# A state-space scan ahead of a feed-forward layer: the first group of tokens, taken as one block or as two halves

## The chip, the cores and the metric

The kernel runs on one core of a Trainium2 chip. The metric is device time in microseconds (us), the median of several executions. A profile is one execution on the same kind of core, recorded instruction by instruction; its "span" runs from the first to the last instruction of the program.

A core has several engines, each with its own instruction stream that it works off in order: TensorE (PE in the profile; its weight loads are listed apart as PEld), VectorE (DVE), ScalarE (ACT), GpSimd (POOL) and SyncE (SP), which here mainly issues DMAs. They meet through semaphores. This kernel fixes the order on every engine by hand: at its end a helper, `in_order`, ties each instruction to the one that the program text emitted before it on the same engine. So a line that stands earlier in the text is earlier in its engine's queue, and an instruction that waits holds up all that stand behind it on that engine.

## The reference, cut to what matters

Two layers in a row. The first (Mamba2, "ssd") works on x (4 batches, 8 heads, 768 tokens, 32 channels), a decay `a` per token and head, and B, C (16 states per token). In chunks, with `state` carried from chunk to chunk:

```python
L = exp(cum_i - cum_j), causal        # decay inside the chunk
y_intra = ((C B^T) * L) @ x           # inside the chunk
y_inter = (C @ state) * exp(cum)      # from the state before the chunk
state = decay_full * state + sum_j B_j x_j decay_from_j
y = y_intra + y_inter
```

The second layer takes y as 3072 tokens by 256 features: `h = y @ w_in` (256 by 2048), `g = h * sigmoid(1.702 h)`, `out = g @ w_out` (2048 by 256). The weights arrive as 64-bit floats and are turned into fp32 on the chip.

## The kernel before, in words

**Tiling.** The 3072 tokens are six groups of 512. A group is two pairs of 256 tokens (`PG` = 2 pairs per group), a pair is two blocks of 128 tokens, and a block has two sides of 64 tokens. So the scan's chunk is 64 tokens here, four chunks per pair, counted m = 0 to 3. Group 0 is handled by code of its own at the start of the kernel; the change touches only that.

**Feed-forward of group 0.** `hidden(0, f)` (L832) is the first product for slice f of 16 slices of 128 hidden features: weight slices `w_in[:, f, k]`, k = 0 and 1, times `yT[0]`, 512 tokens in two halves of 256. fp32 matmuls appear as two records each, so one f is 8 PE records. All 16 run in a row; after a slice a list of other work (`in_hidden[0]`) is emitted. `project_all(0)` is the second product. Later groups use a cheaper scheme for both products, and are not touched.

**Start of group 0**, in the text's order, L1139 to L1169:

- `ends_first` (DVE) scales B. `fetch(1, held=True)` writes one element of the weight buffer on DVE (L171), so that SP's DMA of piece 1 has to wait for it; `fetch(2)` to `fetch(5)` and `rows_a` (the decays of all tokens) follow on SP. The weights come in pieces: 0 to 3 are 512 KB with two slices f each, 4 and 5 are 1 MB with four; pieces 6 to 9 are `w_out`.
- `score` (PE, L640) computes C B^T for both pairs. Between the pairs stand `since_first` (PE L501, ACT L506), the first step of unpacking piece 0 (`unpack`, ACT L197), `weigh(0)` (DVE L651: decay times score), `gain` (PE L671: what each chunk adds to the state, for both pairs) and `parts_first` (ACT L690, four copies 128 x 128 into `steps`).
- Then the second step of `unpack(0)` (ACT L200), `shift(0)` (DVE L204), `weigh(1)`, `drops` (POOL L511: the chunk decays), `since_start` (POOL L625, two: C times decay, "CsT"), and `keep_first` (DVE L695): one scan of 512 elements that turns the increments of all eight chunks into states. `sign(0)` and `join(0)` (DVE L209, L223) finish weight piece 0.
- `dense(2)` (PE L1117) are two matmuls of ones whose result nobody reads.
- `finish(range(PG))` writes y of both pairs into four PSUM banks: first `intra` for pair 0 and pair 1 (L787, 64 records each), then, feature half t by feature half t, `inter` for both pairs (L775, 56 records in all; chunk 0 has no state before it) and two ACT copies (L804) into `yT[0]`.
- `table(AF.Silu)` loads ACT's table, `unpack(2)` and `narrow(1)` (shift, sign, join of piece 1) follow, and `hidden(0, 0)` begins.

PSUM tiles named through `bank` come from four rotating banks, so a new one waits until the reader of the fourth one back is done. `area` is one larger PSUM area with a single buffer.

SP's queue is worked off in the same way: after the pieces come `rows_a`, `fetch(6)` (called by `join(1)`), then the loads for the next group at slice 1 (`load`), and at slice 6 `store_a`, `fetch(7)`, more loads, `fetch(8)`, `fetch(9)`, and at slice 9 the `spread` loads from `scratch`.

Of the kernel before, what the change touches and what calls it, by code (L numbers as in the profile page):

```python
# [8 lines left out]
FP32 = mybir.dt.float32  # L9
U32 = mybir.dt.uint32  # L10
BF16 = mybir.dt.bfloat16
AF = mybir.ActivationFunctionType
# [24 lines left out]
def kernel(  # L37
# [125 lines left out]
    def fetch(i, held=False):  # L163
        name, f, n = PIECES[i]
        if n == 2 and f % 4:
            t = pieces.pop(i - 1)[:, 2 * n * DM:]
        else:
            t = pieces[i] = words(f"bits{i}")
            t = t[:, :2 * n * DM]
        if held:  # L170
            nc.vector.memset(t[:, :1], 0)  # L171
        if name == "in":
            src = moe_w_in[:, 2 * f * P:2 * (f + n) * P].rearrange("(k p) e -> p k e", p=P)
            dst, src = (v.rearrange(s, h=n, e=2 * P) for v, s in (
                (t, "p (h k e) -> k p h e"), (src, "p k (h e) -> k p h e")))
# [278 lines left out]
    def ends_first(p):  # L454

        t = ssd.tile([P, R, 2 * Q, N], FP32, tag="Be", name=f"Be{p}", bufs=3)
        nc.vector.tensor_tensor(
            out=t, in0=rb[p],
            in1=flat[p].rearrange("p r (e i) -> p r e i", i=H)[:, :, :, H - 1:H].to_broadcast(
                [P, R, 2 * Q, N]), op=ALU.mult)  # L460
        BE[p] = t.rearrange("p r (k q) n -> p k r (q n)", k=2), t
# [44 lines left out]
            nc.scalar.activation(since[0][:, 2 * p:2 * p + 2].rearrange("p c s -> p (c s)"),  # L506
                                 rows[p], AF.Exp)

    def drops():

        nc.gpsimd.tensor_copy(  # L511
            drop[:, :, 1:], since[0][:, :CG].rearrange("p c (s i) -> p (c s) i", s=2)[:, 1:, H - 1].unsqueeze(
                1).to_broadcast([P, Q * D, 2 * CG - 1]))

    def fan_since():
        o = bank("rows4")
# [49 lines left out]
    def bank(name):  # L566
        return ps.tile([P, 4 * P], FP32, tag="ff", name=name)

    def area(name):
        return psa.tile([P, R, 4 * P], FP32, tag="cb", name=name)  # L570
# [88 lines left out]
    def gain(pairs, to=None):  # L659
# [16 lines left out]
                            skip_group_check=True)  # L676
            increment[p] = [t[:, 2 * n:2 * n + 2] for t in A] if pairs[0] else A

    steps = const.tile([P, Q * D, 2 * CG], FP32, name="steps")
    drop = ffn.tile([P, 4, TG // 2], FP32, tag="my", name="drop", bufs=1)[:, :2].rearrange(  # L680
        "p a (e m) -> p (a e) m", m=2 * CG)
    nc.gpsimd.memset(drop[:, :, 0:1], 0.0)

    def parts_first():

        to = steps.rearrange("p (q d) (c s) -> p s q c d", s=2, q=Q)
        for i in range(2):
            o = increment[0][i].rearrange("p c (q d) -> p q c d", q=Q)
            for q in range(Q):
                nc.scalar.activation(to[:, i, q], o[:, q], AF.Copy, scale=part[:, q:q + 1])  # L690

    def keep_first():

        flat_steps = steps.rearrange("p e m -> p (e m)")
        nc.vector.tensor_tensor_scan(  # L695
            out=flat_steps, data0=drop.rearrange("p e m -> p (e m)"), data1=flat_steps,
            initial=0.0, op0=ALU.mult, op1=ALU.add)
        for p in range(PG):
            state[p] = steps.rearrange("p e m -> p m e")[:, 4 * p:4 * p + 4]

    def keep_both(pairs, by_scalar=False):

# [25 lines left out]
    def add_up(p, ms):  # L728
        b, c = divmod(2 * p, NC)
        new = state[p]  # L730
        for m in ms:
            if 2 * c + m > 0 and not last_chunk(p, m):
# [4 lines left out]
                    out=new[:, m], in0=old, scalar=since[b][:, c + k, e:e + 1],  # L737
                    in1=new[:, m], op0=ALU.mult, op1=ALU.add)

    begun_y = {}  # L740

    def finish(pairs, steps=range(2)):


        g, first = divmod(pairs[0], PG)
        early = pairs[0] < PG
        if 0 in steps:
            if early:
                y = [bank(f"y0_{i}")[:, :2 * P].rearrange("p (k i) -> p k i", i=H) for i in range(4)]
                begun_y[0] = [[y[2 * t + i] for t in range(NK)] for i in range(2)], set()  # L750
            else:
                both = area(f"y{pairs[0]}")[:, :, :len(pairs) * 2 * H].rearrange(
                    "p (s t) (k i) -> p s t k i", s=2, i=H)
                begun_y[pairs[0]] = [[both[:, i, t] for t in range(NK)] for i in range(2)] + [both], set()
        y, begun = begun_y[pairs[0]]

        def begin(i, t, parts):
            new = not begun & {(i, t, q) for q in parts}
            begun.update((i, t, q) for q in parts)
            return new  # L760

        def inter(n, p, ts=range(2)):

            for k in range(2):
                for i in range(2):
                    m = 2 * k + i
                    if (4 * p + m) % (2 * NC) == 0:
                        continue
                    old = state[p][:, m - 1] if m else state[p - 1][:, 3]
                    for r in range(R):  # L770
                        t = r // 2
                        if t not in ts:
                            continue
                        rows, to = slice(32 * r, 32 * r + 32), Q * D * (r % 2)
                        nc.tensor.matmul(  # L775
                            out=y[i][t][to:to + Q * D, 2 * n + k], lhsT=old[rows],
                            rhs=st[p]["CsT"][rows, k, SIDES[i]],
                            start=begin(i, t, range(Q * (r % 2), Q * (r % 2) + Q)), stop=early,
                            tile_position=(32 * r, to), skip_group_check=True)

        def intra(n, p):
            L = Ls[p]
            for k in range(2):
                for h in range(NH):
                    t, q = divmod(h, HB)
                    for i, side in enumerate(SIDES):
                        nc.tensor.matmul(  # L787
                            out=y[i][t][D * q:D * q + D, 2 * n + k], lhsT=rx[p][side, k, h],
                            rhs=L[side, k, h // Q, h % Q],
                            start=begin(i, t, (q,)), stop=not early, tile_position=(H * i, D * q),  # L790
                            skip_group_check=True)

        cols = slice(2 * first * P, 2 * (first + len(pairs)) * P)

        if first == 0:
            yT[g] = ffn.tile([P, NK, TG], FP32, tag="yT", name=f"yT{g}")
        if early:
            for n, p in enumerate(pairs):
                intra(n, p)
            for t in range(NK):  # L800
                for n, p in enumerate(pairs):
                    inter(n, p, (t,))
                for i in range(2):
                    nc.scalar.activation(  # L804
                        yT[g][:, t, cols].rearrange("p (k s i) -> p s k i", s=2, i=H)[:, i], y[i][t],
                        AF.Copy)
        else:
            for step in steps:
                for n, p in enumerate(pairs):
                    (inter, intra)[step](n, p)  # L810
            if 1 not in steps:
                return
            for i in range(2):
                nc.scalar.activation(  # L814
                    yT[g][:, :, cols].rearrange("p t (k s i) -> p s t k i", s=2, i=H)[:, i], y[2][:, i],
                    AF.Copy)
        for p in pairs:
            state.pop(p - 1, None)
            st.pop(p)
            Ls.pop(p)  # L820
# [5 lines left out]
    def block(g, j):  # L826
        if g or j < 6:
            gT[g, j] = ffn.tile([P, 2, TG], FP32, tag="gT", name=f"gT{g}_{j}", bufs=6)
        else:
            gT[g, j] = ffn.tile([P, 2, TG], FP32, tag="mg", name=f"gT{g}_{j}", bufs=3)  # L830

    def hidden(g, f):  # L832
        j, i = divmod(f, 2)
# [304 lines left out]
    turn_back()  # L1138
    ends_first(0)  # L1139
    ends_first(1)  # L1140
    fetch(1, held=True)
    for i in range(2, 6):
        fetch(i)
    rows_a(az, (nc.sync,))

    def between_scores():
        since_first()
        unpack(0, (0,))
        weigh(0)
        gain(range(PG))  # L1150
        parts_first()

    score(range(PG), between_scores)
    unpack(0, (1,))
    shift(0)
    weigh(1)
    drops()
    for p in range(PG):
        since_start(p, nc.gpsimd)
    keep_first()  # L1160
    sign(0)
    dense(2)
    unpack(1)
    finish(range(PG))
    dense(0)
    join(0)
    table(AF.Silu)
    unpack(2)
    narrow(1)  # L1169


    def at(places, i, *work):
# [46 lines left out]


    for f in range(NF):
        hidden(0, f)
        for do in in_hidden[0].get(f, []):
            do()
    project_all(0, in_project[0])
# [177 lines left out]
```

## Time and profile before

| what | value |
|---|---|
| median of 3 runs | 355.07 us (355.07 to 355.61) |
| the profiled execution: its time / its span | 356.2 / 354.2 us |
| PE / PEld busy | 346.6 (98%) / 300.9 us (85%) |
| DVE / ACT / POOL busy | 241.5 (68%) / 150.0 (42%) / 14.0 us (4%) |
| first matmul of `hidden(0, 0)` starts | 22.07 us |
| 16 slices of `hidden(0, f)`, span of their records | 22.1 to 53.9 us |

The profile has a page (busy shares, the span in forty slices, the chain of work that ended last, the costliest groups) and views of the trace: a timeline for one engine and window, a table by windows with busy time and granted TensorE clock, a view by source line, a view of waits, and the DMA queues. In a timeline row the columns are start, duration, engine, line, operation, output and inputs, shapes, count, and in brackets the idle time before it with what ended it; "issue" there means that the engine waited for nothing that the profile shows.

### The profile page before, as it was taken

The page shows a single profiled execution, that of the slowest core. Times are in us where ns is not written, and L with a number is a line of the kernel's source. Part 1 is how long each engine was busy: PE and PEld are TensorE (multiplying, and loading weights), DVE is VectorE, ACT ScalarE, POOL GpSimd, SP SyncE. Part 2 cuts the span into 40 slices and gives each one's busy share as a digit, 9 for nine tenths or more (in the row PEclk, how much of TensorE's full clock was granted, in tenths as well). Part 3 has the DMA queues.
Part 4 walks back from the last instruction along what each step waited for, and adds up shares of the span by engine and source line. Part 5 has one row for each costly group of instructions (what it writes and reads, how often), then busy time and mean ns, then how long its engine had stood idle before and what let it go on. Part 6 is the DMA issues. An engine that isn't in the chain of part 4 may idle for free.

```text
span 354.2 us, 8373 instructions
## 1 busy us (share of the span) xinstructions
PE 346.6 (98%) x3506; PEld 300.9 (85%) x3506; DVE 241.5 (68%) x453; ACT 150.0 (42%) x346; POOL 14.0 (4%) x42
## 2 busy tenths in 40 slices
PE   8799999999999999999999999999999999999996
PEld 6578888888888888888888888888888888889996
DVE  5635798779867999666898476789374555465463
ACT  4657757013563331654333454333454331553320
POOL 8400000100000100000000000000000000000000
PEclk9969999999999999999999999999999999999999
DMA  6897799552544500415614016400000310000401
GB/s 129 227 304 159 190 241 202 98 89 42 104 71 92 104 0 2 68 41 119 121 30 76 0 34 131 82 11 2 1 4 3 45 16 0 0 2 0 59 2 59
DMA packets 87100, 26.19 MB, mean 74 GB/s; under 512 B 69528, under 2 KB 84248, under 8 KB 87064
## 3 DMA queue, kind: packets, MB, share of 16 engines
q1 hardware_dynamic: 86232, 25.15, 34.4%
q10 hardware_dynamic: 832, 0.52, 0.6%
q8 instruction: 27, 0.44, 0.5%
q14 instruction: 9, 0.07, 0.1%
HBM read 22.41 MB, written 3.24 MB: 72 GB/s over the span
## 4 chain that ended last, share of the span: by engine, by line
PE 88%; DVE 4%; DMA 3%; SPq 2%; issue 2%; ACT 0%; POOL 0%; DVEq 0%; POOLq 0%; ACTq 0%
PE acc L1006 25%; PE X L899 17%; PE Y L909 13%; PE h L843 11%; PE o L943 8%; PE acc L1013 7%; PE y L775 2%; PE y L787 2%; PE cb L640 2%; DMA a<-scratch 1%; DMA bits<-in_moe_w_in_dram 1%; PE A L671 1%; DVE mw L966 1%; DVE gT L1033 1%; SPq L150 1%
## 5 line engine op out<-in xcount | busy, mean ns | idle before, releaser
L904 ACT ACTIVATE ac<-X 128x256 f32<-128x256 f32 x76 | 29.1, 383 | 78.6 <-PE X L899 78.2
L1006 PE MATMUL acc<-mg,mw 128*128 128x256 f32 x192 | 54.5, 379 | 0.0
L876 ACT ACTIVATE gT<-gT 128x512 f32<-128x512 f32 (+1 forms) x76 | 39.3, 519 | 34.3 <-DVE gT L1033 33.7
L1033 DVE TENSOR_TENSOR gT<-Y,ac 128x512 f32<-128x512 f32 x38 | 26.2, 688 | 36.1 <-PE Y L909 30.5
L899 PE MATMUL X<-my,mi 128*128 128x256 f32 x152 | 45.2, 380 | 0.1
L1006 PEld LDWEIGHTS acc<-mg,mw 128*128 128x128 f32 x192 | 36.5, 190 | 5.0
L1033 DVE TENSOR_TENSOR gT<-Y,b 128x256 f32<-128x256 f32 x38 | 15.8, 419 | 34.8 <-PE Y L909 34.8
L843 PE MATMUL h<-yT,w_in 128*128 128x256 f32 (+1 forms) x172 | 38.3, 385 | 0.0
L843 PEld LDWEIGHTS h<-yT,w_in 128*128 128x128 f32 x172 | 32.5, 202 | 4.7 <-ACT S L721 0.2
L1006 PE MATMUL acc<-gT,w_out 128*128 128x256 f32 x128 | 35.5, 379 | 0.0
L899 PEld LDWEIGHTS X<-my,mi 128*128 128x128 f32 x152 | 28.0, 190 | 4.2 <-ACT ac L904 0.5
L943 PE MATMUL o<-gT,w_out 128*128 128x256 f32 x128 | 28.6, 381 | 0.0
L867 DVE TENSOR_TENSOR mg<-gT 128x512 f32<-128x512 f32 x40 | 27.2, 681 | 0.0
L1006 PEld LDWEIGHTS acc<-gT,w_out 128*128 128x128 f32 x128 | 24.2, 190 | 3.4 <-ACT yT L814 0.2
L943 PEld LDWEIGHTS o<-gT,w_out 128*128 128x128 f32 x128 | 24.1, 190 | 3.4
L899 PE MATMUL X<-yT,w_in 128*128 128x256 f32 x76 | 23.2, 389 | 0.0
L904 ACT ACTIVATE b<-X 128x256 f32<-128x256 f32 x38 | 14.6, 384 | 20.0 <-PE X L899 19.5
L909 PE MATMUL Y<-yT,w_in 128*128 128x256 f32 x76 | 22.7, 381 | 0.0
L909 PE MATMUL Y<-my,mi 128*128 128x256 f32 x76 | 22.6, 379 | 0.0
L899 PE MATMUL X<-my,w_in 128*128 128x256 f32 x76 | 22.6, 381 | 0.0
L909 PE MATMUL Y<-yT,mi 128*128 128x256 f32 x76 | 22.5, 379 | 0.0
L391 DVE TENSOR_TENSOR_SCAN L<-a,idents 128x1024 f32<-128x1024 f32 x9 | 20.5, 2278 | 0.5 <-DMA a<-scratch 0.5
(143 smaller groups left out, 531.4 us busy)
## 6 DMA issues: line engine op xcount, KB each, us to landing
a<-scratch SPq DMA_DIRECT2D x18, 256.0 KB, 5.1
bits<-in_moe_w_out_dram SPq DMA_DIRECT2D x8, 512.0 KB, 5.7
x<-in_x_dram SPq DMA_DIRECT2D x24, 128.0 KB, 3.4
out_dram<-ob SPq DMA_DIRECT2D x40, 64.0 KB, 2.0
bits<-in_moe_w_in_dram SPq DMA_DIRECT2D x8, 256.0 KB, 4.8
bits<-in_moe_w_in_dram SPq DMA_DIRECT2D x4, 512.0 KB, 9.1
zC<-in_C_dram SPq DMA_DIRECT2D x40, 32.0 KB, 4.0
zB<-in_B_dram SPq DMA_DIRECT2D x40, 32.0 KB, 2.7
```

The costliest lines, as they stand in the source:

```text
L391: nc.vector.tensor_tensor_scan(out=L, data0=ra[p].rearrange("p k e -> p (k e)"), data1=idents.rearrange("p h i -> p (h i)"), initial=0.0, ...
L640: nc.tensor.matmul(out=s["cb"][side, r, k].rearrange("p (q i) -> p q i", q=Q), lhsT=BT[rows, k, side], rhs=CT[rows, k, :, side], start=Tru ...
L843: nc.tensor.matmul(out=h[:, cols], lhsT=w_in[:, f, k], rhs=yT[g][:, k, cols], start=(k == 0 and e == 0), stop=(k == NK - 1), skip_group_ch ...
L867: nc.vector.tensor_tensor(out=t[:, 0:2], in0=B[:, :, 1], in1=B[:, 0], op=ALU.subtract)
L876: nc.scalar.activation(o, i, AF.Silu, scale=GELU_SCALE / WEIGHT)
L899: nc.tensor.matmul(out=s["X"], lhsT=lhsT, rhs=rhs, start=i == "1", stop=i == "4", skip_group_check=True)
L904: nc.scalar.activation(copy, s["X"], AF.Copy)
L909: nc.tensor.matmul(out=o, lhsT=lhsT, rhs=rhs, start=s.pop("new", False), stop=i != "5", skip_group_check=True)
L943: nc.tensor.matmul(out=o[c][:, cols], lhsT=w_out[:, f, c], rhs=gT[g, f // 2][:, f % 2, cols], start=(f == 0 and e == 0), stop=(f == NF - 1 ...
L1006: nc.tensor.matmul(out=acc[g][0][i][:, cols], lhsT=w, rhs=h[:, cols], start=(j == 0 and k == 0 and (i, 0) in begins), stop=(j == NF // 2 - ...
L1013: nc.tensor.matmul(out=o[k] if type(o) is list else o[:, cols], lhsT=h[:, cols], rhs=w, start=(j == 0 and (i, k) in begins), stop=(j == NF ...
L1033: nc.vector.tensor_tensor(out=o, in0=v, in1=w, op=ALU.add)
```

## The change

Group 0 is no longer one block from `keep_first` on:

- `steps` and `drop` become one tile per pair. Pair 0 has four elements per row, pair 1 has five: the last state of pair 0 is copied in front by ACT (`carry_first`). `drops`, `parts_first` and `keep_first` run once per pair; the increments of pair 0 are scaled by two DVE instructions, those of pair 1 by four ACT copies half as wide as before.
- y of pair 0 is made by `finish_first` (64 records of `intra`, 24 of `inter`, four ACT copies 128 x 128). y of pair 1 goes through the general `finish`, in the PSUM area, with `intra` ahead of `inter` and two ACT copies 128 x 256.
- `hidden(0, 0)` and `hidden(0, 1)` are each cut into the 256 tokens of pair 0 and those of pair 1 (`hidden_half`). The order on PE is: intra and inter of pair 0, half (0, 0), intra and inter of pair 1, half (1, 0), halves (0, 1) and (1, 1), then `hidden(0, 2)` as before.
- `dense(2)` is gone.
- `fetch(1)` is held by a DVE write that stands behind the first scan; `fetch(2)` is now held too, behind `join(0)`. `fetch(3)` to `fetch(5)` and `rows_a` stand behind it on SP.
- Both steps of `unpack(0)` now stand behind the copies of `parts_first(1)` on ACT, and `weigh(1)` stands behind `join(0)` on DVE.

```diff
-    def drops():
+    def drops(p):
...
-    def parts_first():
+    def parts_first(p):
+        to = steps[p][:, :, p:].rearrange("p (q d) (c s) -> p s q c d", s=2, q=Q)
         for i in range(2):
+            o = increment[p][i][:, 2 * p:2 * p + 2].rearrange("p c (q d) -> p q c d", q=Q)
+            if p == 0:
+                nc.vector.tensor_tensor(
+                    out=to[:, i], in0=o,
+                    in1=part.unsqueeze(2).unsqueeze(3).to_broadcast([P, Q, 2, D]), op=ALU.mult)
+                continue
             for q in range(Q):
                 nc.scalar.activation(to[:, i, q], o[:, q], AF.Copy, scale=part[:, q:q + 1])
...
+    def carry_first():
+        nc.scalar.activation(steps[1][:, :, 0], steps[0][:, :, 3], AF.Copy)
...
+    def finish_first():
+        y = [bank(f"y0_{n}")[:, :2 * H].rearrange("p (k i) -> p k i", i=H) for n in range(2 * NK)]
...
+    def hidden_half(f, e):
+        j, i = divmod(f, 2)
+        if e == 0:
+            if i == 0:
+                block(0, j)
+            half_h[f] = bank(f"h0_{f}")
+        cols = slice(e * HT, (e + 1) * HT)
+        for k in range(NK):
+            nc.tensor.matmul(out=half_h[f][:, cols], lhsT=w_in[:, f, k], rhs=yT[0][:, k, cols],
+                             start=(k == 0 and e == 0), stop=(k == NK - 1), skip_group_check=True)
+        if e == 1:
+            nc.scalar.activation(gT[0, j][:, i], half_h[f], AF.Silu, scale=GELU_SCALE / WEIGHT)
...
-    fetch(1, held=True)
-    for i in range(2, 6):
-        fetch(i)
-    rows_a(az, (nc.sync,))
     def between_scores():
         since_first()
-        unpack(0, (0,))
         weigh(0)
         gain(range(PG))
-        parts_first()
+        for p in range(PG):
+            parts_first(p)
     score(range(PG), between_scores)
-    unpack(0, (1,))
-    shift(0)
-    weigh(1)
-    drops()
     for p in range(PG):
+        drops(p)
         since_start(p, nc.gpsimd)
-    keep_first()
-    sign(0)
-    dense(2)
-    unpack(1)
-    finish(range(PG))
-    dense(0)
-    join(0)
-    table(AF.Silu)
-    unpack(2)
-    narrow(1)
+    keep_first(0)
+    fetch(1, held=True)
+    unpack(0)
+    carry_first()
+    finish_first()
+    shift(0)
+    sign(0)
+    join(0)
+    fetch(2, held=True)
+    for i in range(3, 6):
+        fetch(i)
+    rows_a(az, (nc.sync,))
+    table(AF.Silu)
+    weigh(1)
+    keep_first(1)
+    hidden_half(0, 0)
+    unpack(1)
+    finish((1,), (1, 0))
+    hidden_half(1, 0)
+    narrow(1)
+    for f in range(2):
+        hidden_half(f, 1)
+    unpack(2)
...
     for f in range(NF):
-        hidden(0, f)
+        if f > 1:
+            hidden(0, f)
```

More of the change, by code (lines that the diff above doesn't have):

```diff
@@ L507, in since_first @@
                                  rows[p], AF.Exp)
-    def drops():
-        nc.gpsimd.tensor_copy(
-            drop[:, :, 1:], since[0][:, :CG].rearrange("p c (s i) -> p (c s) i", s=2)[:, 1:, H - 1].unsqueeze(
-                1).to_broadcast([P, Q * D, 2 * CG - 1]))
+    def drops(p):
+        ends_of = since[0][:, :CG].rearrange("p c (s i) -> p (c s) i", s=2)[:, :, H - 1]
+        m = slice(1, 4) if p == 0 else slice(4, 8)
+        n = m.stop - m.start
+        nc.gpsimd.tensor_copy(drop[p][:, :, 1:1 + n],
+                              ends_of[:, m].unsqueeze(1).to_broadcast([P, Q * D, n]))
     def fan_since():
@@ L677, in gain, with keep_first @@
             increment[p] = [t[:, 2 * n:2 * n + 2] for t in A] if pairs[0] else A
[L679 to L682, printed above, removed]
-    def parts_first():
-        to = steps.rearrange("p (q d) (c s) -> p s q c d", s=2, q=Q)
-        for i in range(2):
-            o = increment[0][i].rearrange("p c (q d) -> p q c d", q=Q)
+    steps = [const.tile([P, Q * D, 4 + p], FP32, name=f"steps{p}") for p in range(PG)]
+    drop = ffn.tile([P, 4, TG // 2], FP32, tag="my", name="drop", bufs=1).rearrange("p a e -> p (a e)")
+    drop = [drop[:, p * 4 * Q * D:p * 4 * Q * D + (4 + p) * Q * D].rearrange("p (e m) -> p e m", m=4 + p)
+            for p in range(PG)]
+    for p in range(PG):
+        nc.gpsimd.memset(drop[p][:, :, 0:1], 0.0)
+    def parts_first(p):
+        to = steps[p][:, :, p:].rearrange("p (q d) (c s) -> p s q c d", s=2, q=Q)
+        for i in range(2):
+            o = increment[p][i][:, 2 * p:2 * p + 2].rearrange("p c (q d) -> p q c d", q=Q)
[4 more added lines that the diff above has]
+                continue
             for q in range(Q):
                 nc.scalar.activation(to[:, i, q], o[:, q], AF.Copy, scale=part[:, q:q + 1])
-    def keep_first():
-        flat_steps = steps.rearrange("p e m -> p (e m)")
+    def keep_first(p):
+        flat_steps = steps[p].rearrange("p e m -> p (e m)")
         nc.vector.tensor_tensor_scan(
-            out=flat_steps, data0=drop.rearrange("p e m -> p (e m)"), data1=flat_steps,
+            out=flat_steps, data0=drop[p].rearrange("p e m -> p (e m)"), data1=flat_steps,
             initial=0.0, op0=ALU.mult, op1=ALU.add)
-        for p in range(PG):
-            state[p] = steps.rearrange("p e m -> p m e")[:, 4 * p:4 * p + 4]
+        state[p] = steps[p].rearrange("p e m -> p m e")[:, p:]
+    def carry_first():
+        nc.scalar.activation(steps[1][:, :, 0], steps[0][:, :, 3], AF.Copy)
     def keep_both(pairs, by_scalar=False):
@@ L738, in add_up @@
                     in1=new[:, m], op0=ALU.mult, op1=ALU.add)
+    def finish_first():
+        y = [bank(f"y0_{n}")[:, :2 * H].rearrange("p (k i) -> p k i", i=H) for n in range(2 * NK)]
+        for k in range(2):
+            for h in range(NH):
+                t, q = divmod(h, HB)
+                for i, side in enumerate(SIDES):
+                    nc.tensor.matmul(
+                        out=y[2 * t + i][D * q:D * q + D, k], lhsT=rx[0][side, k, h],
+                        rhs=Ls[0][side, k, h // Q, h % Q], start=(k == 0), stop=False,
+                        tile_position=(H * i, D * q), skip_group_check=True)
+        yT[0] = ffn.tile([P, NK, TG], FP32, tag="yT", name="yT0")
+        for t in range(NK):
+            for k in range(2):
+                for i in range(2):
+                    for r in range(2 * t, 2 * t + 2):
+                        m = 2 * k + i
+                        if m == 0:
+                            continue
+                        rows, to = slice(32 * r, 32 * r + 32), Q * D * (r % 2)
+                        nc.tensor.matmul(
+                            out=y[2 * t + i][to:to + Q * D, k], lhsT=state[0][:, m - 1][rows],
+                            rhs=st[0]["CsT"][rows, k, SIDES[i]], start=False, stop=True,
+                            tile_position=(32 * r, to), skip_group_check=True)
+            for i in range(2):
+                nc.scalar.activation(
+                    yT[0][:, t, :2 * P].rearrange("p (k s i) -> p s k i", s=2, i=H)[:, i],
+                    y[2 * t + i], AF.Copy)
+        st.pop(0)
+        Ls.pop(0)
     begun_y = {}
@@ L745, in finish @@
         g, first = divmod(pairs[0], PG)
-        early = pairs[0] < PG
         if 0 in steps:
[L748 to L754, printed above, removed]
+            both = area(f"y{pairs[0]}")[:, :, :len(pairs) * 2 * H].rearrange(
+                "p (s t) (k i) -> p s t k i", s=2, i=H)
+            begun_y[pairs[0]] = [[both[:, i, t] for t in range(NK)] for i in range(2)] + [both], set()
         y, begun = begun_y[pairs[0]]
@@ L760, in begin, with inter @@
             return new
-        def inter(n, p, ts=range(2)):
+        def inter(n, p):
             for k in range(2):
@@ L771, in inter @@
                         t = r // 2
-                        if t not in ts:
-                            continue
                         rows, to = slice(32 * r, 32 * r + 32), Q * D * (r % 2)
@@ L777, in inter @@
                             rhs=st[p]["CsT"][rows, k, SIDES[i]],
-                            start=begin(i, t, range(Q * (r % 2), Q * (r % 2) + Q)), stop=early,
+                            start=begin(i, t, range(Q * (r % 2), Q * (r % 2) + Q)), stop=False,
                             tile_position=(32 * r, to), skip_group_check=True)
@@ L789, in intra @@
                             rhs=L[side, k, h // Q, h % Q],
-                            start=begin(i, t, (q,)), stop=not early, tile_position=(H * i, D * q),
+                            start=begin(i, t, (q,)), stop=True, tile_position=(H * i, D * q),
                             skip_group_check=True)
@@ L796, in finish @@
             yT[g] = ffn.tile([P, NK, TG], FP32, tag="yT", name=f"yT{g}")
-        if early:
+        for step in steps:
             for n, p in enumerate(pairs):
[L799 to L816, printed above, removed]
+                (inter, intra)[step](n, p)
+        if 1 not in steps:
+            return
+        for i in range(2):
+            nc.scalar.activation(
+                yT[g][:, :, cols].rearrange("p t (k s i) -> p s t k i", s=2, i=H)[:, i], y[2][:, i],
+                AF.Copy)
         for p in pairs:
@@ L830, in block @@
             gT[g, j] = ffn.tile([P, 2, TG], FP32, tag="mg", name=f"gT{g}_{j}", bufs=3)
+    half_h = {}
+    def hidden_half(f, e):
[10 more added lines that the diff above has]
+            nc.scalar.activation(gT[0, j][:, i], half_h[f], AF.Silu, scale=GELU_SCALE / WEIGHT)
     def hidden(g, f):
@@ L1140, with between_scores @@
     ends_first(1)
-    fetch(1, held=True)
-    for i in range(2, 6):
+    def between_scores():
+        since_first()
+        weigh(0)
+        gain(range(PG))
+        for p in range(PG):
+            parts_first(p)
+    score(range(PG), between_scores)
+    for p in range(PG):
+        drops(p)
+        since_start(p, nc.gpsimd)
+    keep_first(0)
+    fetch(1, held=True)
+    unpack(0)
[6 more added lines that the diff above has]
+    for i in range(3, 6):
         fetch(i)
     rows_a(az, (nc.sync,))
-    def between_scores():
-        since_first()
-        unpack(0, (0,))
-        weigh(0)
-        gain(range(PG))
-        parts_first()
-    score(range(PG), between_scores)
-    unpack(0, (1,))
-    shift(0)
-    weigh(1)
-    drops()
-    for p in range(PG):
-        since_start(p, nc.gpsimd)
-    keep_first()
-    sign(0)
-    dense(2)
-    unpack(1)
-    finish(range(PG))
-    dense(0)
-    join(0)
-    table(AF.Silu)
+    table(AF.Silu)
+    weigh(1)
+    keep_first(1)
+    hidden_half(0, 0)
+    unpack(1)
+    finish((1,), (1, 0))
[3 more added lines that the diff above has]
+        hidden_half(f, 1)
     unpack(2)
-    narrow(1)
     def at(places, i, *work):
```

## The prediction

> **What bounds the kernel now.** I read the page first. PE is busy 98% of the span and the chain of work that ended last is PE for 88%, so the time can only fall where PE idles, runs below its clock, or does less. The forty slices show where: two at the start.
>
> ```profile
> PE   8799999999999999999999999999999999999996
> PEclk9969999999999999999999999999999999999999
> ```
>
> Each digit is a tenth; slice three (17.7 to 26.6 us) has a granted clock of 0.6. Next the timeline of PE around it:
>
> ```profile
> 13.40 1.13 PE L1117 MATMUL dense<-ones 128*128 128x256 f32 x4
> 14.46 1.49 PE L787 MATMUL y<-L,x 64*32 64x64 f32 x94
> 18.49 0.51 PE L787 MATMUL y<-L,x 64*32 64x64 f32 x34 [2.54 <-issue]
> 18.93 3.21 PE L775 MATMUL y<-CsT,steps 32*64 32x64 f32 x56
> 22.07 10.13 PE L843 MATMUL h<-yT,w_in 128*128 128x256 f32 x33
> ```
>
> PE stops for 2.54 us after 94 of 128 intra records, in the middle of a head, where no semaphore stands; the bracket says "issue". Third, the table by windows (length, then PE, PEld, DVE, ACT, POOL busy, clock, DMA share, GB/s):
>
> ```profile
> 14.00:17.40 3.40, 1.82 (x97) 1.17 (x96) 3.37 (x5) 2.45 (x7) 1.14 (x3) 1.00 0.91 261
> 17.40:20.80 3.40, 2.31 (x72) 2.21 (x73) 2.10 (x4) 0.28 (x2) 0.00 (x0) 1.00 1.02 311
> 20.80:24.20 3.40, 3.40 (x29) 2.92 (x26) 0.00 (x0) 2.72 (x7) 0.00 (x0) 0.50 1.09 355
> 24.20:27.60 3.40, 3.40 (x9) 2.68 (x9) 1.81 (x3) 1.63 (x3) 0.00 (x0) 0.50 1.11 222
> ```
>
> After the stop PE has full clock to 20.8 and half clock for 6.8 us. And the DMA engines are full (0.91 to 1.11) throughout. The DMA view of the window 16 to 17 us holds a row of the queue that carries instructions:
>
> ```profile
> q8 instruction: 1, 0.02, 6.2%
> ```
>
> One packet, one engine's microsecond (6.2% of sixteen). I read the stop as TensorE waiting for its next block of instructions, queued behind weight pieces; the packet moves inside the stop, and the page's 27 such packets, 0.44 MB, come to 63 bytes for each of PE's 7012 instructions, so the queue looks like PE's and a packet (16 KB) like some 260 instructions. After the start the chain shows PE without a gap for tens of us.
>
> The point to beat: by 27.65 us 13 records of hidden have begun (windows by line: "x13" from 22.00 to 27.65), three more at 0.215 us each end the 16 records of f = 0 and 1 near 28.3 us. From there PE is bound by itself.
>
> **The change, step by step.** Times are on the profile's clock.
>
> *First scan.* weigh(0) ends at 12.37 (11.15 + 1.22), the gains at 12.40. Two DVE products of 128 elements: 0.25 us each (L450, 128x128, two in 0.49), to 12.95. drops(0) on POOL has 192 elements where 448 took 0.95: about 0.45, 12.36 to 12.8, covered; CsT(0) 0.8 more (two took 1.61), 13.6. The scan of 256 elements: 0.69 (L334), ends 13.65. Before, it ended at 16.56.
>
> *y of pair 0 on PE.* score ends 13.47; dense (1.06 us from 13.40 to 14.46) is gone. ACT's four copies of A at 64 wide: four of 128 took 1.27; about 0.27 each, so the banks are free at 13.5. Intra: 64 records; 128 took 1.44 us later (83.5 to 85.0), so 0.7 to 0.8, ends 14.4. Inter: 24 records at 57 ns (56 in 3.2 us, same two row groups by turns, a strided state as before): 1.4, ends 15.8. Copies of 128 elements (256 took 0.33 apiece in a row): yT of half t = 0 at 15.9, t = 1 at 16.6.
>
> *Weight piece 0.* unpack(0) now starts on ACT at 13.5 (two at 0.6: 14.1, 14.7); before, it started at 13.04. DVE: shift to 14.7, sign 0.66 to 15.4, join 0.69 to 16.1. Before, 17.87: earlier, since the long scan and weigh(1) no longer precede it. carry_first (one short ACT copy, 0.2 to 0.35) ends near 15.0, needed at 17.3; nothing.
>
> *Half (0, 0).* It waits for join(0): 16.2, four records, 0.86, to 17.1. Behind it in PE's queue is all of pair 1. That waits for weigh(1) anyway: behind join(0), 1.21 us, ends 17.35; the scan of 320 (between 0.69 for 256 and 1.21 for 512: 0.82) ends 18.2.
>
> *y of pair 1.* Intra 17.4 to 18.2. Inter, 32 records over all four row groups: no row for a state with this stride. Bounds are 20 ns (56 records in 1.17 us at 78.7, mostly contiguous state) and 57 ns: 0.6 to 1.8. I take 1.0, since the eight strided records at 78.7 to 78.9 over four row groups ran near the lower row. Ends 19.2. Half (1, 0) covers the copies: 19.2 to 20.1.
>
> *Fetches.* fetch(1) leaves SP at 13.8 and 14.3, where it left at 11.27 and 11.69. Landing took 5.10 us for a 256 KB piece in traffic (7.86 to 12.96) and 3.4 for x, 4.1 for w_out in light traffic; so 17.7 to 19.4, and I take 18.8. On ACT unpack(1) stands ahead of the copies of y: 18.8 to 20.0, then two copies of 256, 0.75, to 20.8. This is what ends last: each us that fetch(1) lands later moves the rest by one. Halves (0, 1) and (1, 1): 20.85 to 22.6. narrow(1) 19.4 to 21.3, covered. fetch(2) leaves at 16.3, lands near 20 to 21, is used at 26. The table load, 1.48 us, runs on ACT from 16.6 to 18.1 while it waits for piece 1.
>
> *The stop and the clock.* If the stop is a wait for instructions in DMA traffic, it goes: if a block is asked for one block (some 260 records) before its use, that is near 12.5 us, when only piece 0 is still moving. With it goes, in my forecast, the half clock. No row of before shows this new pattern: the cost is between nothing and the 6.8 us at half speed, 3.4 us. I take nothing: before, the window 14.0 to 17.4 kept the clock with 1.82 us of PE work, mostly dense, and the one that lost it (17.4 to 20.8) was mostly the thin inter records. After, every such window holds 0.8 to 1.7 us of dense work beside inter.
>
> *Sum.* f = 2 begins at 22.6 where it began at 28.3: 5.7 us.
>
> *What is late next.* DMA. The pieces start 2.6 us later and pause about 1 us between fetch(1) and fetch(2). With DMAs full from 13 to 30 us now, pieces 5 and 6 land 0 to 2 us later, and w_out's and the spread loads behind them on SP, while PE wants them 5.7 us earlier. w_in still suffices: piece 5 landed by 27.7 and f = 12 starts at 39.8 after. In the second product fetch(9) and the spread loads set DVE's order: its only slack there is the 2.86 us in which DVE waits at L736, and narrow(9) ended at 69.4 where f = 12 will be wanted near 71. So 0 to 2 us lost; I take 0.7, nearer to nothing, since SP's later DMAs have landed well before use in the rows I see.
>
> 5.7 less 0.7 is 5.0 us. The profiled execution has 356.2 (span 354.2 and 2.0 around it), so 351.2; the median lies 1.1 lower: **350.1**.
>
> The Trainium skill, page "TensorE: Matmul & The Clock Gate", section "HAM oscillation — how this bites in real kernels", asks only that PE not idle for over about 3.4 us. This trace differs: an idle stretch of 2.54 us among thin work was followed by half clock. By the rule the sum would stand at 5.0 in any case; by the row it may drop by 3.4.
>
> The page "Runtime: NRT & Kernel Launch", section "Instruction fetch mechanics", holds that instruction blocks are prefetched and the cost mostly hidden, which speaks against my reading of the stop. No run here shows another cause; by that rule the 2.54 us would stay, as in the third rival.
>
> **Rivals.**
>
> *The clock falls all the same (20%).* For: PE still works thinly from 14.4 to 16.2 and 18.2 to 19.2, idles some 1 us in pieces, and dense(2) is gone. With half clock from 20.8 to 27.65, 8 records (halves at 16.2 and 19.2) plus 15 (6.6 us at 0.43) are done, 23 against 13: ten at 0.215, 2.1 us. About 353.0.
>
> *Transfers eat the gain (10%).* The loss is 2 us or more and fetch(1) lands at 19.4 to 20: gain 2.5 to 3.5, 352.
>
> *The change doesn't remove the stop (10%).* If it belongs to the instruction stream and not to traffic, it sits at the same instruction count, in pair 1's intra: 17.4 plus 2.54, then half clock as before. PE would then have 4 records done, and 13 more by 27.65: 17 against 13, 0.9 us. About 354.2, half of it within 0.2%.
>
> *Slower (10%).* One mechanism: fetch(1) is starved. Behind it on ACT stand the copies of y, on PE everything. Pieces issued between 15 and 17 us took 10 to 11 us to land in this trace; were that so here (14.3 + 11.2 = 25.5), unpack ends at 26.7, the halves at 29.3, and the long idle costs half clock for 6.8 us, 3.4 more: 32.7 against 28.3, 4 us slower, near 359. It decides from a landing of about 24.5 (without the clock) or 21 (with it). Against it: those pieces had eight others ahead, this one has none.
>
> **How the numbers follow.** Forecast 50%, its own range 348.4 to 351.5 (inter at 0.6 and fetch(1) at 17.7 on one side, 1.8 and 2 us of transfers on the other). The range reaches to the clock's case: 348.4 to 353.8, which leaves out the slower case (10%), some of the third rival (6%) and a bit below (4%). A run can tell about 0.2% (0.7 us) from no change. Faster: 50 + 20 + 10 + 5 = 85%; same 5%; slower 10%.
>
> **What would show it.** In the timeline of PE: no gap over 1 us between 13.5 and 22 us; half (0, 0) near 16.2; f = 2 near 22.6. In the windows: clock 1.00 from 7.2 us on. In the waits: ACT's L197 waiting for bits near 18. In DVE's timeline near 60 us: waits for a or af are the lost 0.7. It is wrong if fetch(1) lands after 20, if the clock reads 0.5 anywhere before 30, or if the "issue" gap comes back at pair 1's intra.

## The result and the profile after

The changed kernel takes 357.33 us (median of 7, 356.44 to 359.11) against 355.07 us (median of 7, 353.78 to 355.92): ratio 1.0075, 95% interval 1.0048 to 1.0102. It is slower; 350.1 was forecast. The profiled execution took 357.15 us, its span is 355.2. Each kernel here has one trace, of one execution, and executions of one kernel differ by up to 5 us, so a time is compared over all of them, and a trace is read for places. On its page the two slices that led the prediction now read:

```profile
PE   8899989969999999999999999999999999999996
PEclk9989999999999999999999999999999999999999
```

The 6 in the clock has become an 8, and PE's row now holds an 8 in the sixth slice (44.4 to 53.3 us) and a 6 in the ninth (71.0 to 79.9 us), where it read 9 before. The timeline of PE over the opening:

```profile
13.10 1.28 PE L759 MATMUL y<-L,x 64*32 64x64 f32 x64
14.32 1.23 PE L772 MATMUL y<-CsT,steps 32*64 32x64 f32 x24
16.57 1.65 PE L868 MATMUL h<-yT,w_in 128*128 128x256 f32 x4 [1.02 <-DVE bits L171]
18.14 1.19 PE L823 MATMUL y<-L,x 64*32 64x64 f32 x64
19.25 1.19 PE L811 MATMUL y<-CsT,steps 32*64 32x64 f32 x32
20.38 2.86 PE L868 MATMUL h<-yT,w_in 128*128 128x256 f32 x12
```

Slice f = 2 begins at 23.07 us, where 16 records of hidden had ended near 28.3 us before. So the opening gives 5.2 us. The same timeline later:

```profile
68.71 0.55 PE L673 MATMUL A<-x,Be 64*32 64x64 f32 x32 [0.88 <-DVE Be L450]
69.19 5.45 PE L984 MATMUL o<-gT,w_out 128*128 128x256 f32 x24
75.41 1.99 PE L984 MATMUL o<-gT,w_out 128*128 128x256 f32 x8 [0.78 <-DVE w_out L223]
79.55 0.45 PE L811 MATMUL y<-CsT,steps 32*64 32x64 f32 x8 [2.15 <-DVE L L653]
```

In this last row the first states of pair 2 are put to use. Before, it read:

```profile
78.71 0.47 PE L775 MATMUL y<-CsT,steps 32*64 32x64 f32 x8
```

So between 23 and 80 us the kernel lost 5.2 plus 0.8, 6.0 us. Of these, 1.1 us stand in no gap; matmuls follow each other more slowly there (the last 40 records of `hidden` take 9.22 us, in e1 below 8.90). The view of waits of PE from 45 to 100 us names the other 4.9 (before, this view is empty for the same stretch):

```profile
PE y L811 <- DVE L L653: 2.1, 1, 2.1
PE o L984 <- ACT gT L888: 1.1, 1, 1.1
PE A L673 <- DVE Be L450: 0.9, 1, 0.9
PE o L984 <- DVE w_out L223: 0.8, 1, 0.8
```

The columns are us in total, times, longest. PE waits for VectorE and ScalarE; what do these wait for? The waits of ACT (36 to 75 us) and of DVE (36 to 100 us):

```profile
ACT m L197 <- DMA bits<-in_moe_w_out_dram: 12.5, 3, 6.3
...
DVE m L204 <- ACT m L197: 8.4, 3, 4.7
DVE L L391 <- DMA a<-scratch: 2.5, 1, 2.5
```

Transfers. Before, ACT waited for none there. The tile of DVE's scan L391 comes by the `spread` loads (`a<-scratch`); what DVE makes behind it is what that last row of PE waits for. DVE before, then after:

```profile
60.12 2.29 DVE L391 TENSOR_TENSOR_SCAN L<-a,idents 128x1024 f32<-128x1024 f32 x1
72.30 0.33 DVE L736 SCALAR_TENSOR_TENSOR S<-steps,since,S 128x64 f32<-128x64 f32 x1 [2.86 <-ACT S L721]
74.32 2.35 DVE L651 TENSOR_TENSOR L<-L,cb 128x1024 f32<-128x1024 f32 x2
```

```profile
66.04 2.29 DVE L391 TENSOR_TENSOR_SCAN L<-a,idents 128x1024 f32<-128x1024 f32 x1 [2.48 <-DMA a<-scratch]
75.27 0.32 DVE L748 SCALAR_TENSOR_TENSOR S<-steps,since,S 128x64 f32<-128x64 f32 x1
77.06 2.35 DVE L653 TENSOR_TENSOR L<-L,cb 128x1024 f32<-128x1024 f32 x2
```

Before, DVE had time to spare on this way (2.86 us ahead of L736, and `weigh` ended at 76.67, 2 us ahead of its use); after, it has none.

And the transfers are late from the start. The table by windows (last two columns DMA share and GB/s) shows the DMA engines with nothing to do between piece 0 and piece 1; first the kernel before, then after:

```profile
12.00:14.00 2.00, 1.89 (x67) 1.45 (x64) 0.62 (x2) 1.26 (x5) 1.64 (x3) 1.00 0.78 228
14.00:15.00 1.00, 0.87 (x27) 0.38 (x31) 1.00 (x2) 1.00 (x5) 1.00 (x3) 1.00 0.91 233
```

```profile
12.00:14.00 2.00, 1.79 (x103) 1.32 (x86) 1.82 (x5) 1.46 (x6) 2.00 (x4) 1.00 0.06 14
14.00:15.00 1.00, 1.00 (x52) 0.91 (x33) 0.87 (x3) 0.92 (x3) 0.82 (x2) 1.00 0.00 0
```

### The profile page after: what moved, and what is told of

It is laid out like the page before. It is cut to its first block, busy times and chain, and to the rows that moved or that the text cites. A ratio compares the mean times of both kernels' runs of the same rounds, so it can differ in the third digit from the quotient of the medians.

```text
span 355.2 us, 8374 instructions
## 1 busy us (share of the span) xinstructions
PE 344.0 (97%) x3502; PEld 297.3 (84%) x3502; DVE 242.8 (68%) x457; ACT 149.9 (42%) x349; POOL 14.3 (4%) x44
## 4 chain that ended last, share of the span: by engine, by line
PE 83%; DVE 8%; DMA 6%; issue 1%; ACT 1%; SPq 1%; POOL 0%; DVEq 0%; POOLq 0%
PE acc L1047 25%; PE X L940 17%; PE Y L950 13%; PE h L884 9%; PE acc L1054 7%; DMA af<-in_a_dram 3%; PE y L823 2%; PE y L811 2%; PE o L984 2%; PE cb L642 1%; DMA a<-scratch 1%; PE h L868 1%; PE A L673 1%; DMA x<-in_x_dram 1%; PE busy L429 1%
## 5 line engine op out<-in xcount | busy, mean ns | idle before, releaser
L945 ACT ACTIVATE ac<-X 128x256 f32<-128x256 f32 x76 | 29.1, 383 | 78.6 <-PE X L940 78.2
L1047 PE MATMUL acc<-gT,w_out 128*128 128x256 f32 x128 | 35.5, 379 | 0.0
L884 PE MATMUL h<-yT,w_in 128*128 128x256 f32 (+1 forms) x156 | 32.4, 365 | 0.1
L884 PEld LDWEIGHTS h<-yT,w_in 128*128 128x128 f32 x156 | 27.3, 190 | 4.2 <-PE h L884 0.5
L945 ACT ACTIVATE b<-X 128x256 f32<-128x256 f32 x38 | 14.6, 384 | 19.8 <-PE X L940 19.3
L391 DVE TENSOR_TENSOR_SCAN L<-a,idents 128x1024 f32<-128x1024 f32 x9 | 20.5, 2278 | 3.1 <-DMA a<-scratch 3.1
L950 PE MATMUL Y<-my,mi 128*128 128x256 f32 x76 | 22.6, 379 | 0.0
L940 PE MATMUL X<-my,w_in 128*128 128x256 f32 x76 | 22.6, 381 | 0.0
```

The costliest lines, as they stand in the source:

```text
L391: nc.vector.tensor_tensor_scan(out=L, data0=ra[p].rearrange("p k e -> p (k e)"), data1=idents.rearrange("p h i -> p (h i)"), initial=0.0, ...
L884: nc.tensor.matmul(out=h[:, cols], lhsT=w_in[:, f, k], rhs=yT[g][:, k, cols], start=(k == 0 and e == 0), stop=(k == NK - 1), skip_group_ch ...
L940: nc.tensor.matmul(out=s["X"], lhsT=lhsT, rhs=rhs, start=i == "1", stop=i == "4", skip_group_check=True)
L945: nc.scalar.activation(copy, s["X"], AF.Copy)
L950: nc.tensor.matmul(out=o, lhsT=lhsT, rhs=rhs, start=s.pop("new", False), stop=i != "5", skip_group_check=True)
L1047: nc.tensor.matmul(out=acc[g][0][i][:, cols], lhsT=w, rhs=h[:, cols], start=(j == 0 and k == 0 and (i, 0) in begins), stop=(j == NF // 2 - ...
```

## The experiments

Theory A: the transfers of the first group are a chain of their own, nearly as long as PE's; the change starts it later, and what the opening gives is lost where PE catches up with it. Theory B: the halves themselves cost it, by more small work on VectorE and ScalarE, or by the clock. All are variants of the changed kernel unless said otherwise. e1 to e4, e5 to e7 and e8 to e10 each ran beside runs of the kernel before (medians 354.66, 355.24 and 354.95 us), so across these groups the ratios compare, not the microseconds.

**e1, halves without late loads.**

```diff
+    fetch(1, held=True)
+    for i in range(2, 6):
+        fetch(i)
+    rows_a(az, (nc.sync,))
     def between_scores():
...
     keep_first(0)
-    fetch(1, held=True)
...
-    fetch(2, held=True)
-    for i in range(3, 6):
-        fetch(i)
-    rows_a(az, (nc.sync,))
```

> The changed kernel, but all weight loads (pieces 1 to 5) and the load of the decays stand on SP and DVE where they stood before the change. Theory A (the first group's chain of transfers is the second bound, and the change only starts it later): the second half of piece 5 lands near 28 us instead of 32.4, that of piece 9 near 56 to 58 instead of 63.1, TensorE's waits in the second product (4.9 us in all) fall below 1.5 us, and the ratio to the kernel before is 0.984 to 0.993. Theory B (the halves themselves, with their order on VectorE and ScalarE, cost later what they give at the start): the transfers come earlier and the time stays at 356.5 to 358. Under both the stop of TensorE for instructions can come back in pair 1's intra with 0 to 2.5 us.

Measured: 353.72 us (350.85 to 355.53), ratio 0.9953, interval 0.9922 to 0.9983. Piece 5 lands at 27.1 us, piece 9 at 57.2. The waits of PE from 60 to 85 us hold one row:

```profile
PE y L811 <- DVE L L653: 0.3, 1, 0.3
```

f = 2 begins at 23.03, as in the changed kernel: in these two executions, which both read half clock for 3.4 us there, the late loads gave the opening nothing. The same halves, with the loads put back, turn a loss into a gain. But the gain is small: the ratio is outside the expected 0.984 to 0.993, 0.47% is 1.7 us of the 5.2 that the opening gives. The traced execution took 351.5 us, 2.2 below the median of its kernel; no trace shows where the seven executions of 353.3 to 355.5 us lose the rest.

**e2, piece 1 early, pieces 2 to 5 behind the first scan.**

```diff
+    fetch(1, held=True)
     def between_scores():
...
     keep_first(0)
-    fetch(1, held=True)
+    fetch(2, held=True)
+    for i in range(3, 6):
+        fetch(i)
+    rows_a(az, (nc.sync,))
```

> The changed kernel, with piece 1 loaded at its place before the change and pieces 2 to 5 held behind the first scan, so without the pause between pieces 1 and 2. Theory A: piece 5 lands near 30 us, piece 9 near 59 to 60, TensorE's waits in the second product fall to 1 to 3 us, ratio 0.99 to 1.00, no stop for instructions. Theory B: 356.5 to 358 as the changed kernel.

Measured: 355.60 us, ratio 1.0029, interval 1.0006 to 1.0053. Piece 5 at 30.4, piece 9 at 60.9; no stop; f = 2 at 21.73. But PE waits 4.6 us in the second product, not 1 to 3. The clock read 1.00 throughout the opening here, so PE also arrived 1.3 us earlier than in the changed kernel. In place between e1 and the changed kernel, as A has it (its interval just touches the changed kernel's); the ratio is above the expected 0.99 to 1.00, and the size of the waits was underrated.

**e3, the kernel before with the late loads alone.**

```diff
-    fetch(1, held=True)
-    for i in range(2, 6):
-        fetch(i)
-    rows_a(az, (nc.sync,))
...
     keep_first()
+    fetch(1, held=True)
     sign(0)
     dense(2)
-    unpack(1)
+    join(0)
+    fetch(2, held=True)
+    for i in range(3, 6):
+        fetch(i)
+    rows_a(az, (nc.sync,))
     finish(range(PG))
     dense(0)
-    join(0)
     table(AF.Silu)
+    unpack(1)
     unpack(2)
```

> The kernel before, in one block, with the late loads alone: piece 1 held behind the scan, pieces 2 to 5 and the decays behind join of piece 0, and unpacking of piece 1 behind the copies of y. Theory A: the stop of 2.54 us is gone and slice f = 2 begins at 24 to 26 instead of 28.3 us, but piece 5 lands at 33 to 35 and piece 9 at 63 to 66, and the time is 357 to 360. Theory B: the loads cost nothing, and without stop and halves the time is 350 to 352.

Measured: 359.89 us, ratio 1.0133, interval 1.0099 to 1.0167. Piece 5 lands at 35.5, piece 9 at 66.8. The timeline of PE, in the place of the 2.54 us of "issue":

```profile
15.84 0.86 PE L787 MATMUL y<-L,x 64*32 64x64 f32 x64 [0.31 <-DVE L L651]
17.07 3.21 PE L775 MATMUL y<-CsT,steps 32*64 32x64 f32 x56 [0.37 <-DVE bits L171]
20.20 17.14 PE L843 MATMUL h<-yT,w_in 128*128 128x256 f32 x72
```

Hidden starts at 20.2 instead of 22.1 us, f = 2 at 25.09 instead of near 28.3. So the stop does go when the traffic goes, as predicted, and the kernel is still 1.3% slower. The half clock did not go with it: it read 0.5 from 19.5 to 22.9 us, behind thin records with no gap over 0.4 us. The two parts nearly add up: e1's 0.47% down and e3's 1.33% up make 0.86% up; the whole change is 0.75% up. (It is not an exact sum: the scan of one block ends later, so piece 5 lands 3 us later here than in the changed kernel.)

**e4, the 1 MB of piece 7 left out.**

```diff
         name, f, n = PIECES[i]
+        if i == 7:
+            bits[7] = bits[6]
+            return
```

> The changed kernel without the 1 MB transfer of piece 7: its slices of the second weight matrix are unpacked a second time from piece 6, so all arithmetic is done and only the transfer is left out. Theory A: the loads behind it on SP land about 3 us earlier (piece 9 near 60), TensorE's waits in the second product fall from 4.9 to under 2 us, time 352.5 to 355. Theory B: waits and time stay, 356.5 to 358.

Measured: 353.24 us, ratio 0.9958, interval 0.9932 to 0.9984: with the late loads kept, less traffic takes away 1.2%. The profile agrees less well: piece 9 lands at 61.6 (60 expected) and PE's waits from 45 to 100 us fall from 4.9 to 3.3 us, not under 2. It is of the slowest of the ten executions (356.31 us), in which the clock was at half for 3.4 us at 78. The direction is A's, the arithmetic on the engines being the same. (The kernel leaves out a part of `w_out`, so its output is not the layer's.)

**e5, two matmuls of ones ahead of half (0, 0).**

```diff
+    dense(2)
     hidden_half(0, 0)
```

> The changed kernel with two matmuls of ones put back, into the 1.0 us in which TensorE waits for piece 0 ahead of half (0, 0). Theory A: the half clock of 3.4 us near 17 us goes, slice f = 2 begins at 21.7 to 22.3 instead of 23.1, but the second product still waits for the late transfers, so the time stays within 1 us of the changed kernel (356 to 358). Theory B (the clock at the start is what costs): 353 to 355.

Measured: 358.79 us, ratio 1.0098, interval 1.0077 to 1.0120. The clock reads 1.00 through the opening and f = 2 begins at 22.29 instead of 23.07; the time is no better than the changed kernel's, and above the expected 356 to 358. So 0.8 us gained at the start were lost behind it as well, which is what A says and B's clock cannot.

**e6, e1 with the same filler.** The diff is e5's, put into e1.

> The kernel of e1 (halves, loads where they stood before) with the same two matmuls of ones ahead of half (0, 0). Theory A: clock 1.00 through the start, f = 2 at 21.7 to 22.3, transfers as in e1, TensorE waits in the second product 0.5 to 1.5 us, 350.5 to 352.5, ratio 0.988 to 0.993, and less spread than e1's 350.9 to 355.5. Theory B (in e1 the gain came from the loads alone and the clock is no part of it): 353.7 as e1.

Measured: 353.40 us (351.30 to 355.70), ratio 0.9940, interval 0.9913 to 0.9967: not to be told from e1, as theory B had it here. Clock 1.00 in the opening, f = 2 at 22.51. What theory A expected failed: f = 2 and the time came later, the spread did not shrink, PE waited 1.7 us for `weigh`, and the stop for instructions came back, at the place that the prediction's third rival had named:

```profile
16.33 1.10 PE L868 MATMUL h<-yT,w_in 128*128 128x256 f32 x4
17.36 0.24 PE L823 MATMUL y<-L,x 64*32 64x64 f32 x1
17.97 0.84 PE L823 MATMUL y<-L,x 64*32 64x64 f32 x63 [0.36 <-issue]
```

One record of pair 1's intra, then 0.36 us of "issue". The packet of instructions moved at 15.7 us here; in the changed kernel, with idle DMA engines, it moved at 13.5 and there was no stop. A second stop of 0.74 us stands at 81.5 us; e7 has both too (0.50 and 0.67 us).

**e7, e6 with piece 8 ahead of pair 3's loads.**

```diff
-    at(in_hidden[0], 6, store_a, lambda: fetch(7), lambda: load(PG + 1), lambda: fetch(8))
+    at(in_hidden[0], 6, store_a, lambda: fetch(7), lambda: fetch(8), lambda: load(PG + 1))
```

> The kernel of e6 with piece 8's load moved on SP ahead of the twelve loads for pair 3. Theory A: piece 8 lands near 46 to 48 instead of 52.7, ScalarE no longer waits for it (3.1 us in e1), the loads for pair 3 land 3 us later; TensorE waits the same or less, time 0 to 1 us below e6. If the loads for pair 3 (B and x of the scan) are what the second product waits for, the time is 1 to 3 us above e6.

Measured: 353.39 us, ratio 0.9948, interval 0.9924 to 0.9973, as e6. Piece 8 landed at 45.4, and VectorE then waited 5.7 us for the spread tile instead of 2.8. Piece 8 was not what was late; ScalarE now waited for piece 9 instead (4.1 us).

**e8, e6 with the spread loads ahead of piece 9.**

```diff
-    NEXT = {1: (6,), 5: (9,)}
+    NEXT = {1: (6,)}
...
-    at(in_hidden[0], 9, lambda: spread(PG + 1), lambda: spread_rows(1))
+    at(in_hidden[0], 6, lambda: spread(PG + 1), lambda: spread_rows(1))
+    at(in_hidden[0], 9, lambda: fetch(9))
```

> The kernel of e6 with the spread loads of pair 3 and the row of decays moved on SP ahead of piece 9. Theory A (in the second product VectorE waits for these, and piece 9 behind them has slack): in e6 the spread tile was waited for by 2.8 us; here it lands near 55 to 57, VectorE's scan at L391 starts at 58 to 59 instead of 61.3, TensorE's wait for weigh (1.7 us at L811) falls below 0.5, time 350.5 to 352, ratio 0.985 to 0.991. If piece 9, now later by 3 to 4 us, is what is late, TensorE waits for it at f = 12 and the time is that of e6 or up to 2 us more.

Measured: 351.65 us (350.60 to 355.05), ratio 0.9929, interval 0.9902 to 0.9957. The spread tile lands at 57.3. The timeline of DVE:

```profile
58.92 0.68 DVE L324 TENSOR_TENSOR idents<-ident 128x512 f32<-128x512 f32 x1
59.64 2.29 DVE L391 TENSOR_TENSOR_SCAN L<-a,idents 128x1024 f32<-128x1024 f32 x1
```

The scan no longer waits for a transfer; it starts behind its neighbour, which waited for piece 8. PE's wait is down from 1.7 to 1.0 us (under 0.5 expected), and the ratio is a little above the expected 0.985 to 0.991. This is the best of the kernels tried, below the one before with its whole interval; its interval overlaps those of e1, e6 and e7, so how much of it is this step's is not settled.

**e9, e8 with pieces 3 to 5 held behind the first scan.**

```diff
     fetch(1, held=True)
-    for i in range(2, 6):
-        fetch(i)
-    rows_a(az, (nc.sync,))
+    fetch(2)
...
     keep_first(0)
+    fetch(3, held=True)
+    for i in range(4, 6):
+        fetch(i)
+    rows_a(az, (nc.sync,))
```

> The kernel of e8 with pieces 1 and 2 at their early place and only pieces 3 to 5 and the decays held, behind the first scan. Theory A: the queue holds enough to stay busy (no pause), so later transfers land within 1 us of e8's, while fewer pieces lie ahead of TensorE's block of instructions: the stop at the head of pair 1's intra (0.4 to 0.7 us in e6) goes, f = 2 begins at 21.5 to 22. Time 0 to 0.8 us below e8. If the hold still costs, pieces 4 and 5 land over 1.5 us later and the time is 1 to 2 us above e8.

Measured: 353.97 us, ratio 0.9963, interval 0.9933 to 0.9994. Piece 5 lands at 29.1 instead of 26.6, PE waits 4.6 us from 45 to 100 instead of 1.0, the span of the profiled execution is 353.5 instead of 348.6. So a hold of about 1 us (piece 3 leaves at 13.5 instead of 12.5) makes later loads late too, and there was no stop in e8's profile for it to remove. That it costs time is likely and not settled: the medians are 2.3 us apart, but the intervals overlap, and the profiled executions are the fastest of e8's twelve and the second slowest of e9's.

**e10, e9 without the filler.** The two matmuls are taken out.

> The kernel of e9 without the two matmuls of ones. If they keep the clock, it reads 0.5 for 3.4 us near 17 in this kernel, f = 2 begins 0.8 to 1.3 us later than in e9, and the time is 0.5 to 1.3 us above e9's. If the clock holds without them, the time is e9's.

Measured: 353.86 us, ratio 0.9951, interval 0.9923 to 0.9979, as e9. In the profiled execution the clock stayed at 1.00 without the filler, and f = 2 began at 22.08 against 21.81. It tells nothing on the filler's worth: the clock's windows fell at other times than in e1 (see the end).

Set side by side, the landing of pieces 5 and 9 and of the spread tile, the start of the row in which PE puts the first states of pair 2 to use, PE's waits from 45 to 100 us and the ratio:

| kernel | piece 5, us | piece 9, us | spread tile, us | first states of pair 2, us | PE waits, us | ratio to before |
|---|---|---|---|---|---|---|
| before | 27.7 | 55.2 | 58.95 | 78.71 | none | 1 |
| e1 | 27.1 | 57.2 | 60.30 | 73.94 | 0.3 | 0.9953 |
| e2 | 30.4 | 60.9 | 64.03 | 77.66 | 4.6 | 1.0029 |
| changed | 32.4 | 63.1 | 65.92 | 79.55 | 4.9 | 1.0075 |
| e3 (no halves) | 35.5 | 66.8 | 68.85 | 82.47 | 4.9 | 1.0133 |

e1, e2 and the changed kernel have the same halves and differ in the loads alone; the time follows the transfers. The traces show the way: in the four kernels below the first row, PE's row starts 13.61 to 13.64 us after the spread tile has landed (e4, e5 and e6 too), so that this landing, and not PE's opening, set the time there. Before, it was 19.8 us: 6.1 us lay spare. (In e8 to e10 piece 9 stands elsewhere in the queue and can't be compared.)

## Why the prediction was wrong

It was wrong in the sign, and by one step, "What is late next". The late loads account for 1.2% of the 2.1% between forecast and result; the rest stays open (last point).

- **The opening was right.** Half (0, 0) at 16.2 forecast, 16.57 measured; fetch(1) landed 18.8, 18.4; f = 2 at 22.6, 23.07; gain 5.7, 5.2. Inter of pair 1 took 1.19 us for 32 records (37 ns each, between the bounds of 20 and 57).
- **The stop was read rightly.** It is gone in the changed kernel and in e3, and comes back in e6 and e7 where the traffic does, at a place set by the count of instructions: PE stops after the same 705 recorded instructions (weight loads included) before, in e6 and in e7, and the second stop of e6 and e7 is 1280 instructions and five packets on, 256 a packet where the prediction had some 260. PE passes its 449th instruction, one packet ahead of the stop, 3.3 us before the packet moves in the kernel before, and 1.1 us before it moves in the changed kernel with its idle DMA engines. That the engine waits for its own instructions is still read off these times, not shown by itself. Nor does the traffic alone decide: e8 begins as e6 does, its packet moved 1.5 us sooner, and there was no stop. But the hold was not needed for it: in e1, with all the traffic, PE came to that place at 18.1 us, after the block.
- **The clock was half right.** Not 1.00 throughout as forecast: it read 0.5 once, for 3.4 us instead of 6.8. The price, by e5, was 0.8 us at f = 2, where the step allowed up to 3.4 and the rival's 353.0 is 2.9 over the forecast. The wait of 1.02 us for join(0) stood ahead of it, but such a wait does not decide it: e1 lost the clock with one of 1.01 us, e2 and e10 kept it with 0.92 and 1.00. Nor does the half clock go with the stop, as forecast: e3 has no stop and lost it. And the window that the step leaned on (14.0 to 17.4) was not "mostly dense": the dense matmuls end at 14.53, the other 1.4 us are thin records of intra, and it kept the clock.
- **"What is late next" failed.** The step reads: pieces 5 and 6 land 0 to 2 us later, "So 0 to 2 us lost; I take 0.7". Measured: piece 5 4.7 us later (27.65 to 32.39), piece 6 4.4, piece 8 6.1, piece 9 7.9, the spread tile 7.0 (58.95 to 65.92), and 6.0 us lost. Three faults in it. First, the start: I charged fetch(1)'s 2.6 us and a pause of 1 us, but all from piece 2 on hang on the second hold, and piece 2 left SP at 16.47 instead of 12.20: 4.3 us. Second, a full queue has no slack to take that up. I had read the DMA share of 0.9 to 1.1 from 13 to 30 us, and used it as a reason for a small loss; it is the reason for passing the whole shift on. SP's queue is in order, so every later load came with it. (Why pieces 8 and 9 and the spread tile came 1.9 to 3.6 us later still is not traced.) Third, the slack at the other end was not added up: "SP's later DMAs have landed well before use" was not so for the one that counted, which landed at 58.95 and was used at 60.12, and the 2.86 us at L736 was not DVE's only slack. With those two and the 2 us behind `weigh`, 6.1 us lay between landing and PE's need. A need 5.2 us earlier fits into that, as e1 shows (landing 1.4 us later, 0.3 us of waiting); a landing 7.0 us later on top of it does not: 5.2 and 7.0 less 6.1 is 6.1, and 6.0 was lost. For narrow(9) I compared with its old end, 69.4; it ended at 75.35, since the scan ahead of it in DVE's queue started 5.9 us later.
- **The rival "transfers eat the gain"** had the mechanism, with 10% and a gain of still 2.5 to 3.5 us. Its price followed the step above, so it could not reach the other side. The slower rival (fetch(1) starved) was another mechanism and did not happen.
- **The range** does not follow from the terms named beside it: 0.4 and 1.1 us less, or 0.8 and 1.3 us more, than 350.1 are 348.6 and 352.2, not 348.4 and 351.5.
- **Open.** Without the late loads the ratio is still 0.9953 (e1), where 350.1 would be 0.986. e1's traced execution (351.5 us) is as forecast for the profiled one (351.2), its median (353.72) is not. What the slower executions lose, and whether the halves have a part in it as theory B has it, no trace shows.

## What to carry to other kernels

When PE is made to arrive earlier somewhere, lay the transfers beside it as a second chain: for each load after that point, landing time against time of use, and follow the work from there to PE, with its idle time added. The smallest such sum (here 6.1 us, of which 1.2 at the load itself) is what can be gained before the loads must move too. A hold on an in-order queue is paid by every load behind it: here 4.3 us on piece 2, in a full queue, came out as 4.4 to 7.9 us on pieces 6 to 9. If a hold is meant to let one packet through, look first whether something else already moved its need back. And a step that undoes its own cause (here halves, which gave the instruction block 2 us more) should be tried without the second remedy.

## What the runs showed of the hardware that was not expected

- The granted clock changed only at times 3.41 us (or a multiple) apart: before, it read 1.0 for 13.65 us, then 0.5 for 6.83; in the changed kernel 1.0 for 10.24, then 0.5 for 3.41. This grid lies elsewhere in each execution: the first grant of full clock on record stands at 4.5 us (e10), 5.2 (e8), 6.7 (changed) and 7.2 us (before). The same stretch of thin work kept the clock in one run and lost it in another: e10's opening, with a wait of 1.00 us, kept it, e1's, with one of 1.01, did not. e8's twelve runs fall into eight at a mean clock of 1.00 (350.6 to 352.6 us) and four at 0.995 (353.5 to 355.1); that the clock makes this difference is not shown, since none of the four was traced and e1 has 0.995 beside 351.5 us as well as 355.2.
- Matmul records with strided states came every 57 ns over two row groups by turns (L775, before, 56 in 3.21 us), and every 36 ns over four (L811, 32 records in 1.14 us with full clock in e5).
- The packets of instructions, 16 KB each, took 0.9 to 1.9 us on their one DMA engine, and before, PE went on 1.4 us after its packet had moved (17.1 to 18.5 us), in e6 and e7 1.3 and 1.5 us.
